# Another order for the first unit of an attention and maxout kernel, with other masks, loads and weight conversion

## The chip, the cores and the metric

The kernel runs on one core of a Trainium2 chip. The metric is the device time of one execution in microseconds (us); lower is better. Engines are named as the profile names them: PE is TensorE (matmuls), DVE is VectorE, ACT is ScalarE, POOL is GpSimd, and SP is SyncE, which here only issues DMAs.

## What is computed

Three stages follow each other: banded attention (4 batches, 8 heads, 576 positions, 64 wide; half of the heads see the last 32 positions, half see every fourth of the last 128), a maxout layer, and a layer with a rational function.

```python
scores = np.where(masks, q @ k.T / 8, -1e9)           # per head
attn = exp(scores - max) / (sum + 1e-9);  x = attn @ v  # (2304, 512)
h = np.maximum(np.maximum(x @ w1, x @ w2), x @ w3)      # (2304, 768)
x = h @ w_out                                           # (2304, 512)
h = x @ w_in                                            # (2304, 2048)
g = (a0 + a1*h + a2*h**2 + a3*h**3) / (1 + abs(b0*h) + abs(b1)*h**2 + 1e-6)
out = g @ w_out2                                        # (2304, 512)
```

The weights arrive as 64-bit floats, and the kernel makes 32-bit ones out of their bits.

## The kernel before, in words

**Tiling.** The 2304 tokens are twelve attention chunks of 192 (c = 0 to 11). Two chunks are a unit u of 384 tokens. For each of the six units `moe1(u)` runs 18 maxout groups (6 values of f by j = 0, 1, 2) and then four output groups `wo1`. Each product is made from high and low halves: per 128 rows of depth three matmuls, high by high, high by low, low by high (`mm3`). A maxout group is 12 matmuls with 384 columns, a wo1 group 18. While unit u is in `moe1`, the attention of unit u + 1 is woven in between. After the six units comes the rational layer.

**Attention of a chunk** has two kinds of heads, p (plain) and d (dilated), and the steps S (scores on PE, with the mask added by a matmul for the first four chunks), MX (row maximum on DVE), E (exponential on ACT, for the first four chunks one instruction per 64 or 48 rows, with the sum read out of an accumulator), SB (division by the sum, DVE), X (transposes on PE and a copy), V (times the values on PE), and VE (split into x1h by ACT and x1l by DVE).

**Conversion of a weight tile** (128x512, 24 tiles for `moe1`): `load`, `abs` on ACT, three passes `bits` on DVE, `hi` on ACT, `lo` on POOL. The `abs` result lives in a buffer `cvt`, of which there are four in unit 0; `lo` frees it. A group of PE reads a tile's `hi` first and its `lo` in its third matmul. In unit 0 and 1 POOL also makes `hl`, the low half of the maxout result. In units 1 to 4, 32 tiles of the last layer's weights are converted and stored by POOL's DMA queue (`w2d`), with two `cvt` buffers.

**Order.** The string START lists by hand what happens before `moe1(0)`, the two chunks of unit 0 and S2:p of unit 1. W:n are n matmuls on zeros that only keep PE busy. Each engine runs its own instructions in that order. All later steps are ordered by a scheduler. All input loads, also those of later chunks, are issued by SP; the load of chunk c + 2's queries stands behind the scores of chunk c, in whose buffer it lands.

## Time and profile before

| | |
|---|---|
| median of 3 runs | 841.38 us (840.77 to 842.07) |
| the profiled execution | 840.17 us, of it 838.4 us span |
| PE busy | 808.7 us (96%) |
| DVE busy | 646.2 us (77%) |
| ACT busy | 488.5 us (58%) |
| POOL busy | 133.8 us (16%) |

The span lies inside the time of the execution, 1.8 us are around it. Busy time is an average over stages; how full an engine is in a stage is read from a table of windows. The granted clock of TensorE is given as a share of 2.4 GHz.

### The profile page before, as it was taken

Reading aid. Unit: us, or ns where it says so; the run is one execution under the profiler, and the core shown is the slowest. Engines: PE = TensorE matmul, PEld = TensorE weight load, DVE = VectorE, ACT = ScalarE, POOL = GpSimd, SP = SyncE. Lnnn points to the kernel's source line nnn. Section 1 sums busy time; section 2 is a strip of 40 time slices with the busy share of each in tenths; the row PEclk is TensorE's granted clock in tenths of the full one; section 3 lists DMA queues with packets and bytes.
Section 4 is the critical chain, followed back from the end, with each engine's and each line's share of the span. In section 5 each row is a group of like instructions: output and inputs, shape, how many; then the busy total and the mean of one; then the engine's idle time right before and its main releaser. Section 6 shows DMA issues by size and latency. Waiting matters only on the chain.

```text
span 838.4 us, 13171 instructions
## 1 busy us (share of the span) xinstructions
PE 808.7 (96%) x4965; PEld 750.4 (89%) x4965; DVE 646.2 (77%) x1172; ACT 488.5 (58%) x1023; POOL 133.8 (16%) x145
## 2 busy tenths in 40 slices
PE   7889789999999999999989999999999999999998
PEld 5688689999999999999988899999999999999996
DVE  4689937657758657636349899999999999998996
ACT  3565622333333333325449788788778778777775
POOL 0156431220010010016860000000000000000000
PEclk9699889999999999999999999999999999999999
DMA  8784313664555544444620002002002001000001
GB/s 284 233 303 152 148 59 119 207 209 156 171 168 160 191 151 127 153 140 150 207 95 1 1 1 76 1 0 76 2 1 76 0 1 38 1 2 7 31 1 38
DMA packets 29439, 82.54 MB, mean 98 GB/s; under 512 B 3904, under 2 KB 7488, under 8 KB 29376
## 3 DMA queue, kind: packets, MB, share of 16 engines
q1 hardware_dynamic: 24080, 64.66, 24.0%
q0 software_dynamic: 5296, 17.04, 5.5%
q8 instruction: 39, 0.64, 0.3%
q14 instruction: 24, 0.20, 0.1%
HBM read 63.87 MB, written 17.83 MB: 97 GB/s over the span
## 4 chain that ended last, share of the span: by engine, by line
PE 86%; issue 5%; POOL 3%; ACT 3%; DVE 3%; DMA 1%; SPq 0%; POOLq 0%; ACTq 0%; DVEq 0%
PE mm L505 10%; PE mm L506 10%; PE mm L504 10%; PE acc L780 8%; PE acc L778 8%; PE acc L779 8%; PE h L505 8%; PE h L504 8%; PE h L506 8%; PE sc L289 3%; POOL w1s L487 2%; PE tpp L345 2%; PE pv L371 1%; PE pv L365 1%; POOL wo1s L487 1%
## 5 line engine op out<-in xcount | busy, mean ns | idle before, releaser
L506 PE MATMUL mm<-x1h,w1s 128*128 128x384 f32 x432 | 147.0, 340 | 3.6 <-POOL w1s L487 3.6
L504 PE MATMUL mm<-x1h,w1s 128*128 128x384 f32 x432 | 149.3, 347 | 0.4 <-ACT w1s L479 0.4
L505 PE MATMUL mm<-x1l,w1s 128*128 128x384 f32 x432 | 146.7, 340 | 1.0 <-DVE x1l L387 1.0
L504 PE MATMUL h<-x2h,w2s 128*128 128x384 f32 x384 | 129.6, 337 | 3.8 <-DVE p L739 3.8
L505 PE MATMUL h<-x2l,w2s 128*128 128x384 f32 x384 | 129.9, 338 | 0.0
L506 PE MATMUL h<-x2h,w2s 128*128 128x384 f32 x384 | 129.8, 338 | 0.0
L778 PE MATMUL acc<-w2s,gh 128*128 128x512 f32 x288 | 113.6, 394 | 0.0
L779 PE MATMUL acc<-w2s,gh 128*128 128x512 f32 x288 | 113.4, 394 | 0.0
L780 PE MATMUL acc<-w2s,gl 128*128 128x512 f32 x288 | 110.3, 395 | 0.0
L729 ACT ACTIVATE q<-h 128x384 f32<-128x384 f32 x96 | 47.2, 491 | 77.6 <-PE h L506 76.2
L736 DVE SCALAR_TENSOR_TENSOR q<-q,cs,ab 128x384 f32<-128x384 f32 x96 | 67.5, 704 | 29.5 <-ACT ab L730 29.4
L506 PEld LDWEIGHTS mm<-x1h,w1s 128*128 128x128 f32 x432 | 82.5, 191 | 5.2 <-POOL w1s L487 5.2
L505 PEld LDWEIGHTS mm<-x1l,w1s 128*128 128x128 f32 x432 | 82.5, 191 | 2.2 <-DVE x1l L387 2.2
L504 PEld LDWEIGHTS mm<-x1h,w1s 128*128 128x128 f32 x432 | 82.3, 191 | 1.3 <-ACT w1s L479 0.7
L504 PEld LDWEIGHTS h<-x2h,w2s 128*128 128x128 f32 x384 | 72.6, 189 | 8.0 <-DVE p L739 4.1
L505 PEld LDWEIGHTS h<-x2l,w2s 128*128 128x128 f32 x384 | 72.5, 189 | 3.8
L506 PEld LDWEIGHTS h<-x2h,w2s 128*128 128x128 f32 x384 | 72.6, 189 | 0.3
L523 DVE TENSOR_TENSOR m<-mm,m 128x384 f32<-128x384 f32 x72 | 39.8, 553 | 42.7 <-PE mm L506 38.8
L731 ACT ACTIVATE p<-h,cs 128x384 f32<-128x384 f32 x96 | 65.1, 678 | 0.0
L780 PEld LDWEIGHTS acc<-w2s,gl 128*128 128x128 f32 x288 | 54.1, 188 | 12.0
L745 ACT ACTIVATE r<-q,cs 128x384 f32<-128x384 f32 x96 | 59.6, 621 | 5.1 <-DVE q L736 4.6
L779 PEld LDWEIGHTS acc<-w2s,gh 128*128 128x128 f32 x288 | 54.1, 188 | 9.4
(90 smaller groups left out, 1588.9 us busy)
## 6 DMA issues: line engine op xcount, KB each, us to landing
w1r<-in_w_dram SPq DMA_DIRECT2D x18, 512.0 KB, 7.5
raw<-in_w_in_dram SPq DMA_DIRECT2D x16, 512.0 KB, 3.8
w2d<-cvt POOLq DMA_DIRECT2D x32, 256.0 KB, 3.4
...
x2d<-xs POOLq DMA_DIRECT2D x24, 192.0 KB, 2.4
```

The costliest lines, as they stand in the source:

```text
L487: nc.gpsimd.tensor_sub(slot[:, 512:1024], t, slot[:, 0:512].bitcast(F32))
L504: nc.tensor.matmul(o, lhsT=lh, rhs=rh, start=(i == 0), stop=False)
L505: nc.tensor.matmul(o, lhsT=lh, rhs=rl, start=False, stop=False)
L506: pe_at[0] = nc.tensor.matmul(o, lhsT=ll, rhs=rh, start=False, stop=(i == n - 1))
L523: nc.vector.tensor_tensor(out=t, in0=o, in1=t, op=ALU.max)
L729: nc.scalar.activation(out=s["q"], in_=s["h"], func=AF.Square)
L731: nc.scalar.activation(out=s["p"], in_=s["h"], func=AF.Identity, scale=cs[:, 3:4], bias=cs[:, 2:3])
L736: nc.vector.scalar_tensor_tensor(out=s["q"], in0=s["q"], scalar=cs[:, 5:6], in1=s["ab"], op0=ALU.mult, op1=ALU.add)
L745: nc.scalar.activation(out=s["r"], in_=s["q"], func=AF.Ln, scale=LS, bias=cs[:, 6:7])
L778: nc.tensor.matmul(o, lhsT=gh, rhs=w[:, 0:512], start=(c == 0), stop=False)
L779: nc.tensor.matmul(o, lhsT=gh, rhs=w[:, 512:1024], start=False, stop=False)
L780: nc.tensor.matmul(o, lhsT=gl, rhs=w[:, 0:512], start=False, stop=(c == F2 - 1))
```

## The change

It has five parts.

1. START is replaced by another list. It has one block W:14 at its head and no later W, runs the scores of both chunks first, splits E, X and VE into smaller steps (D, E, SM; X, XC; VH, VL), and goes on into `moe1(0)`: H:n is the first half (192 columns, chunk 0) of group n, P:n the second half or, from n = 3, the whole group, M, HH and HL what follows on ACT and DVE. It ends behind the sixth group.
2. The masks and the identity come as bf16 constants in two small loads (`mask16`, `maskd16`), and the fp32 identity in one; the three casts go.
3. Loads: in the first unit SP issues only loads into fresh tiles. The queries of chunks 2 to 11, the keys of batches 1 to 3, the values of chunks 2 to 11 and the coefficients go to POOL's queue.
4. A weight's sign and exponent come from one ACT pass (`up`, Prelu with slope -2^32 in place of Abs), so that `bits` has two DVE passes instead of three. `lo` and all `hl` go from POOL to DVE. `cvt` has three buffers instead of four.
5. E writes sums through the accumulator only where EXPS says "A" (0:p, and chunks 2 and 3); chunk 1 sums on DVE, and 0:d uses one subtraction on DVE and one exponential. SB of 0:p multiplies on ACT, six instructions.

```diff
 START = """
-W:7
-S0:p v:0 L:3 S0:d MX0:p E0:p MX0:d S1:p W:2
...
+W:14 kp0 mk16 qp0 kd0 qd0 mkd16 kp1 qp1 qd1 L:1 ident L:1 v0 L:1 L:1 v1 L:1 L:1 L:1 L:1 L:1 rest
+S0:p,sc MX0:p E0:p S0:d,mm MX0:d S1:p,pv D0:d E0:d SB0:p,act SM0:d S1:d,mm MX1:p SB0:d E1:p
...
+VL1:d up VL1:p H:1 up bits up P:0 hi bits P:1 lo hi bits M:0 up H:2 M:1 hi bits P:2 lo hi M:2
+P:3 lo HH:0 HL:0 lo P:4 M:3 M:4 P:5 M:5 HH:1 HL:1
 """
...
-    ACT_UNITS = 4
+    EXPS = {"0:p": "A", "1:p": "C", "1:d": "C", "2:p": "A", "2:d": "A", "3:p": "A", "3:d": "A"}
     MASK_PE = 4
-    HL_POOL = 2
...
-    CVT = 4
+    CVT = 3
...
         if part is None:
-            nc.sync.dma_start(out=kTp, in_=src)
+            nc.gpsimd.dma_start(out=kTp, in_=src)
+            nc.gpsimd.dma_start(out=kTd.rearrange("p n m -> p (n m)"), in_=kd_in[b])
...
+        queue = nc.sync if c < QA else nc.gpsimd
...
+        queue = nc.sync if c < 2 else nc.gpsimd
...
-        nc.scalar.activation(out=t, in_=cv[i][1].bitcast(F32), func=AF.Abs, scale=SHRINK)
+        nc.scalar.activation(out=t, in_=cv[i][1].bitcast(F32), func=AF.Prelu, scale=SHRINK,
+                             alpha=-(2.0 ** 32))
...
-        elif part == 1:
-            nc.vector.scalar_tensor_tensor(out=t, in0=high, scalar=SIGN, in1=t,
-                                           op0=ALU.bitwise_and, op1=ALU.bitwise_or)
...
-            nc.gpsimd.tensor_sub(slot[:, 512:1024], t, slot[:, 0:512].bitcast(F32))
+            nc.vector.tensor_sub(slot[:, 512:1024], t, slot[:, 0:512].bitcast(F32))
...
-                    (nc.gpsimd if u < HL_POOL else nc.vector).tensor_sub(hl, t, hh.bitcast(F32))
```

On ACT, at the start of the program, before the change (sb are the exponentials, spare the same for chunk 1 in the change; pt is a copied transpose, x1h the split result, cvt the weight tile in work, w1s a finished one):

```order
L320 ACTIVATE sb_186,sm_188<-sc_174,mx_187 128x96 x3
L320 ACTIVATE sb_186,sm_188<-sc_175,mx_187 128x96 x3
L320 ACTIVATE sb_217,sm_219<-sc_199,mx_218 96x48 x4
L320 ACTIVATE sb_217,sm_219<-sc_200,mx_218 96x48 x4
L449 ACTIVATE cvt_294<-w1r0_0_193 128x512
L386 ACTIVATE x1h0_172<-pv_278 128x2x192
```

On ACT, at the same place, in the change:

```order
L361 ACTIVATE sb_218,sm_220<-sc_206,mx_219 128x96 x3
L361 ACTIVATE sb_218,sm_220<-sc_207,mx_219 128x96 x3
L357 ACTIVATE sb_248<-sb_248 96x8x48
L379 ACTIVATE sb_218<-sb_218,sm_220 128x96 x6
L361 ACTIVATE spare_203<-sc_253,mx_265 128x96 x3
L361 ACTIVATE spare_203<-sc_254,mx_265 128x96 x3
L397 ACTIVATE pt_319<-tpp_314 48x384
L361 ACTIVATE spare_203<-sc_279,mx_293 96x80 x4
L361 ACTIVATE spare_203<-sc_280,mx_293 96x80 x4
L397 ACTIVATE pt_363<-tpp_328 96x384
L503 ACTIVATE cvt_365<-w1r0_0_174 128x512
L432 ACTIVATE x1h0_204<-pv_343 128x2x4x48
```

The first split result (x1h) now stands behind the exponentials of both chunks, and the eight exponentials of 0:d are one.

On DVE, in the second value of f of `moe1(0)`, in the change (tile names: 533 is conversion tile 5, 629 is 6, 650 is 7, 671 is 8; a row that writes w1s is a `lo`):

```order
L511 SCALAR_TENSOR_TENSOR cvt_533<-w1r1_2_193,cvt_533 128x512
L533 TENSOR_TENSOR w1s1_0_527<-cvt_492,w1s1_0_527 128x512
L509 TENSOR_SCALAR cvt_629<-cvt_629 128x512
L511 SCALAR_TENSOR_TENSOR cvt_629<-w1r2_0_195,cvt_629 128x512
L533 TENSOR_TENSOR w1s2_0_668<-cvt_629,w1s2_0_668 128x512
L509 TENSOR_SCALAR cvt_650<-cvt_650 128x512
L511 SCALAR_TENSOR_TENSOR cvt_650<-w1r2_1_197,cvt_650 128x512
L533 TENSOR_TENSOR w1s2_1_677<-cvt_650,w1s2_1_677 128x512
L571 TENSOR_TENSOR m_531<-mm_535,m_531 128x384
L533 TENSOR_TENSOR w1s1_1_549<-cvt_496,w1s1_1_549 128x512
L509 TENSOR_SCALAR cvt_671<-cvt_671 128x512
```

Before, the `lo` steps stood on POOL, in the order in which PE reads the tiles:

```order
L487 TENSOR_TENSOR w1s1_0_542<-cvt_494,w1s1_0_542 128x512
L487 TENSOR_TENSOR w1s1_1_578<-cvt_503,w1s1_1_578 128x512
L528 TENSOR_TENSOR hl0_603<-m_523,hh0_602 128x384
L487 TENSOR_TENSOR w1s1_2_606<-cvt_545,w1s1_2_606 128x512
L487 TENSOR_TENSOR w1s2_0_668<-cvt_581,w1s2_0_668 128x512
L487 TENSOR_TENSOR w1s2_1_692<-cvt_609,w1s2_1_692 128x512
```

In the change the `lo` of w1s1_1 stands behind those of w1s2_0 and w1s2_1. In the built program the cvt tiles 492, 629, 650 and 671 have one address, so each of them waits for the `lo` of the one before.

POOL's queue at the start, in the change (before, POOL held two casts there and no load):

```order
L648 DMA co_141<-in_a_dram 128x4
L649 DMA co_141<-in_b_dram 128x2
L232 DMA qTp2_216<-in_qp_dram 128x768
L235 DMA qTd2_242<-in_qd_dram 128x768
L217 DMA kTp1_244<-in_kp_dram 128x1152
L218 DMA kTd1_245<-in_kd_dram 128x1152
L232 DMA qTp3_263<-in_qp_dram 128x768
```

These loads now run beside SP's. On PE the last 3572 rows, from inside the wo1 part of unit 0 to the end, are the same before and after apart from buffer numbers.

## Rows read from the trace of the kernel before

**Rows 1.** Windows: us; busy PE, PEld, DVE, ACT, POOL; granted clock; DMA share; GB/s.
```profile
0.00:39.40 39.40, 31.20 (x258) 22.56 (x258) 20.76 (x53) 18.34 (x81) 3.42 (x8) 0.86 0.80 264
39.40:111.90 72.50, 59.81 (x413) 54.71 (x411) 66.98 (x98) 44.31 (x112) 41.03 (x28) 0.90 0.54 189
...
128.90:189.00 60.10, 59.86 (x469) 58.55 (x468) 40.62 (x72) 20.86 (x39) 13.11 (x18) 1.00 0.56 186
...
440.00:838.00 398.00, 393.67 (x1956) 354.89 (x1956) 364.02 (x688) 306.36 (x604) 8.02 (x15) 1.00 0.05 19
```

**Rows 2.** Timeline of PE: start, length, instruction, idle before it and releaser.
```profile
7.82 0.66 PE L280 MATMUL sc<-mP,ident 128*128 128x288 bf16 x2 [3.33 <-POOL ident L589]
...
37.50 1.95 PE L371 MATMUL pv<-pt,vd 80*64 80x48 f32 x32
39.38 0.69 PE L504 MATMUL mm<-x1h,w1s 128*128 128x384 f32 x1
...
55.89 0.69 PE L506 MATMUL mm<-x1h,w1s 128*128 128x384 f32 x1 [1.80 <-POOL w1s L487]
...
59.26 0.36 PE L504 MATMUL mm<-x1h,w1s 128*128 128x384 f32 x1
...
71.16 1.14 PE L371 MATMUL pv<-pt,vd 80*64 80x48 f32 x32
...
124.54 0.33 PE L504 MATMUL mm<-x1h,w1s 128*128 128x384 f32 x1
...
186.87 0.44 PE L504 MATMUL mm<-x1h,w1s 128*128 128x384 f32 x1
```

**Rows 3.** The chain that ended last, around 115 us: start, length, what.
```profile
112.56 0.32 PE mm L504
...
120.02 0.17 PE mm L504
```

**Rows 4.** Timeline of DVE, 44 to 48 us.
```profile
44.19 0.69 DVE L462 SCALAR_TENSOR_TENSOR cvt<-w1r,cvt 128x512 int32<-128x512 int32 x1
44.80 0.42 DVE L459 TENSOR_SCALAR cvt<-cvt 128x512 int32<-128x512 int32 x1
45.13 0.69 DVE L465 SCALAR_TENSOR_TENSOR cvt<-w1r,cvt 128x512 int32<-128x512 int32 x1
...
46.33 0.55 DVE L523 TENSOR_TENSOR m<-mm,m 128x384 f32<-128x384 f32 x1
46.80 1.65 DVE L465 SCALAR_TENSOR_TENSOR cvt<-w1r,cvt 128x512 int32<-128x512 int32 x1
```

**Rows 5.** Timeline of POOL at the same time.
```profile
46.62 1.28 POOL L487 TENSOR_TENSOR w1s<-cvt,w1s 128x512 fp32r<-128x512 f32 x1 [2.76 <-ACT w1s L479]
```

**Rows 6.** Timeline of ACT: first exponentials, and a conversion.
```profile
11.79 0.34 ACT L320 ACTIVATE sb<-sc,mx 128x96 f32<-128x96 f32 x1 [9.77 <-DVE mx L312]
12.03 0.19 ACT L320 ACTIVATION_READ_ACCUMULATOR sb<-sc,mx 128x1 f32 x1
12.12 0.33 ACT L320 ACTIVATE sb<-sc,mx 128x96 f32<-128x96 f32 x1
...
26.06 0.66 ACT L479 ACTIVATE w1s<-cvt 128x512 fp32r<-128x512 f32 x1
26.59 0.68 ACT L449 ACTIVATE cvt<-w1r 128x512 f32<-128x512 f32 x1
27.14 0.51 ACT L349 ACTIVATE pt<-tpp 96x384 f32<-96x384 f32 x1
```

**Rows 7.** Windows of 2 us, columns as in rows 1.
```profile
18.00:20.00 2.00, 2.00 (x37) 1.83 (x36) 1.94 (x9) 1.42 (x5) 0.00 (x0) 1.00 1.01 407
...
26.00:28.00 2.00, 0.30 (x3) 0.30 (x4) 1.67 (x2) 1.65 (x4) 1.19 (x1) 1.00 1.08 246
28.00:30.00 2.00, 1.30 (x8) 0.63 (x6) 1.90 (x5) 1.73 (x9) 0.07 (x1) 0.64 1.01 276
```

**Rows 8.** DMA issues on the page: count, KB each, median us to landing.
```profile
x2d<-xs POOLq DMA_DIRECT2D x24, 192.0 KB, 2.4
```

More of the change, by code (lines that the diff above doesn't have):

```diff
@@ L190, with bank @@
     at_k = {}
+    done_v = {}
+    def bank(pool, name):
+        if pool == "tp":
+            return tp_p.tile([128, 512], F32, tag="tp", name=name)
+        if pool == "sc":
+            return sc_p.tile([128, 512], F32, tag="sc", bufs=2, name=name)
+        return (mm_p if pool == "mm" else pv_p).tile([128, 512], F32, tag=pool, name=name)
     x1 = {}
+    spare = []
     def load_k(b, part=None):
@@ L243, in attn_pieces @@
         kTp, kTd = at_k[b]
+        if c == 0:
+            spare.append(com.tile([128, NP * TU], F32, tag="x1h", bufs=2, name="spare"))
         if part == 0:
@@ L408, in attn @@
             for word in row.replace("-", "").split():
-                word = word.replace("a:", f"{2 * u}:").replace("b:", f"{2 * u + 1}:")
-                if word not in done_words:
-                    do(word)
+                op, _, arg = word.partition(":")
+                for part in parts.get(op[:-1], (op[:-1],)):
+                    do(f"{part}{2 * u + (op[-1] == 'b')}:{arg}")
             yield
@@ L506, in mm3, with m1_mm @@
             pe_at[0] = nc.tensor.matmul(o, lhsT=ll, rhs=rh, start=False, stop=(i == n - 1))
+    m1 = {}
+    def m1_mm(u, f, j, cols=slice(0, TU)):
+        if (u, f, j) not in m1:
+            m1[u, f, j] = mm_p.tile([128, 512], F32, tag="mm", name="mm")[:, 0:TU]
+        x1h, x1l = x1[u]
+        w = w1s[f, j]
+        mm3(m1[u, f, j][:, cols], [(w[:, 128 * c:128 * c + 128], w[:, 512 + 128 * c:640 + 128 * c],
+                                    x1h[:, c, cols], x1l[:, c, cols]) for c in range(KC)])
@@ L530, in moe1 @@
+                if ("P", u, f, j) not in m1_done:
+                    m1_mm(u, f, j)
+                if ("M", u, f, j) not in m1_done:
+                    m1_max(u, f, j)
+                if j == 2 and ("HH", u, f) not in m1_done:
+                    m1_hh(u, f)
+                if j == 2 and ("HL", u, f) not in m1_done:
+                    m1_hl(u, f)
                 yield ("h", f, j)
+        hs = [m1["h", u, f] for f in range(F1)]
         for c in range(KC):
@@ L618 @@
                         cv_step("load")
-                elif op == "v":
-                    load_v(int(arg))
+                elif op in loads:
+                    loads[op]()
                 elif op == "W":
-                    busy(*[x if x.isalpha() else int(x) for x in arg.split(",")])
-                elif op[0] == "b" and op[1:].isdigit():
-                    assert cv_at["bits"] < cv_at["abs"]
-                    cv_bit(cv_at["bits"], int(op[1:]))
-                    cv_at["bits"] += op == "b2"
+                    busy(int(arg))
+                elif op == "H":
+                    m1_mm(0, 0, int(arg), slice(0, CH))
+                elif op == "P":
+                    f, j = divmod(int(arg), 3)
+                    m1_mm(0, f, j, slice(CH if (0, f, j) in m1 else 0, TU))
+                    m1_done.add(("P", 0, f, j))
+                elif op == "M":
+                    f, j = divmod(int(arg), 3)
+                    m1_max(0, f, j)
+                    m1_done.add(("M", 0, f, j))
+                elif op in ("HH", "HL"):
+                    f = int(arg)
+                    (m1_hh if op == "HH" else m1_hl)(0, f)
+                    m1_done.add((op, 0, f))
                 elif op in steps:
@@ L630 @@
                     do(word)
-                    done_words.add(word)
         cs = const.tile([128, 8], F32, name="cs")
```

258 lines of the change are left out of this document (139 added, 119 removed).

## The prediction, made before the result

> **What bounds the kernel now.** I read the windows by stage first. From 128.9 us on PE is busy 59.86 of 60.10 us, and in the last layer 393.67 of 398.00, both at full clock [rows 1]. There only fewer or faster matmuls could help, and the change leaves PE's rows from unit 0's wo1 part to the end as they are. So the gain can only come from the time up to 124.54, where PE begins the first group of unit 1 [rows 2].
>
> That time has two parts. Up to 39.38 [rows 2] attention of two chunks is done step after step, with PE partly on dummy matmuls. From 39.38 to 124.54, 85.2 us, PE does unit 0. What would that cost at full clock? Matmuls with 384 columns follow each other every 0.17 us [rows 3]; alternating 0.17 and 0.18 makes 0.1735. Unit 0 has 18 x 12 + 4 x 18 = 288 of them, 50.0 us. Unit 1 takes 62.3 us (124.54 to 186.87 [rows 2]), so attention woven in costs 12.4 us. Unit 0 thus lost some 23 us to waits and half clock.
>
> The reason is DVE: 66.98 busy us of 72.50 [rows 1]. Its instructions there are of two lengths. Undisturbed, a two-input pass over 128x512 takes 0.61 us from start to start (44.19 to 44.80), the one-input pass 0.33 (44.80 to 45.13), a 128x384 pass 0.47 (46.33 to 46.80) [rows 4]. But the pass that starts at 46.80 lasts 1.65 us [rows 4], and POOL's `lo` runs from 46.62 to 47.90 [rows 5]: the pass ends about 0.6 us after POOL does. Such pairs repeat through the stage. POOL's 41 busy us there [rows 1] cost DVE time of its own.
>
> **When unit 0 can start.** The first score matmul starts at 7.82, after a wait for POOL's cast of the identity [rows 2]. The change has no cast and 160 KB less ahead of this step. I take 1 us off: 6.8. Before, the first exponential came 4.0 us later, at 11.79 [rows 6], with the scores at half clock; fourteen dummy matmuls right up to them should keep the clock, which saves some 1.2 us. First exponential: 9.6.
>
> From there ACT carries the chain. An exponential with accumulator takes 0.33 us (11.79 to 12.12), without one at most 0.24 (11.79 to 12.03); a 512-wide pass takes 0.54 (26.06 to 26.59 to 27.14), and a 384-wide one, 0.51 long [rows 6], some 0.45 in a row. In the change's order ACT does, up to the last x1h of chunk 1: 6 exponentials with accumulator (2.0), one wide one (0.4), 6 + 6 + 8 + 2 short ones (5.2), ten copies or splits (4.5), four conversion passes (2.1): 14.2 us. Without any wait that ends at 23.8. Of this, 8.3 us stand ahead of the first split, at 17.9, and it needs V0:d.
>
> V0:d needs the values of chunk 0. The loads up to them on SP's queue are 4.5 MB. At the 407 GB/s of a full DMA stretch [rows 7] that is 11 us, at 264, the mean of the first stage [rows 1], 17: alone they land between 12 and 18. But POOL's queue sends queries 2 and keys 1 (2.0 MB) at the same time; all of it ahead costs 4.8 us more, so 12 to 23. I take 20, nearer to the shared case, as the DMA engines are full in that stretch. That is 20 + 1.95 for V0:d at half clock [rows 2] = 22.0, 4 us later than ACT wants it. Half clock because PE then idles: before, PE was busy only 0.30 us between 26 and 28, and the clock granted fell to 0.64 in the next window [rows 7]; the 1.95 at 37.50 against 1.14 at 71.16 for the same V step [rows 2] is its price. The V steps of chunk 1 at half clock add some 1.5. H:0, the first group, starts at 23.8 + 4 + 1.5 = **29.3** instead of 39.38; bounds 24 and 33.
>
> The Trainium skill, "DMA: Bandwidth & Descriptors", section "SWDGE vs HWDGE vs iDMA", says that a DMA engine takes turns between the queues fed by POOL and those fed by SP. No row of before has both at once. With strict turns the values would land at about 22, and the total would be 2 us higher.
>
> **Unit 0 from there.** Matmuls: 50.0 us. Three groups are cut into halves of 192 columns; a half lies between half of 0.1735 and all of it, so the cut costs 0 to 6 us. Weight loads of the same size keep up with about 0.1 us in the score steps, so I take 0.1: 1.1 us. Attention of chunks 2 and 3: 12.4, less S2:p (1.5, done ahead), more six mask matmuls (0.8): 11.7.
>
> DVE loses one pass of three per tile (24 x 0.61 = 14.6 us) and gains `lo` and `hl` (24 x 0.61 + 6 x 0.47 = 17.5). That is 3 us more, but POOL no longer computes, so its passes are all undisturbed: per tile 0.33 + 0.61 + 0.61 = 1.55 us.
>
> **A new wait.** On DVE the `lo` of w1s1_1 stands behind those of tiles 6 and 7, and these two, like tile 8, use the one buffer that tile 3 frees. So they run one after the other: `up` 0.54, `bits` 0.94, `hi` 0.54, `lo` 0.61, with hand-overs 3.0 us each, and DVE has nothing else in its queue. From H:0 at 29.3: x1l of chunk 1 is done at 30.3; then three tiles' bits and one `lo` (3.4), SB2:p (1.0), a maximum that waits for group 1 (to 36.2), bits and `lo` of tile 3 (37.8), tiles 6 and 7 (43.8), a maximum (44.3), the `lo` of w1s1_1 (44.9). PE has by then done six halves and group 3 (6 x 1.2 + 2.1, and 1.6 for half clock, from 29.3: 40.2) and two matmuls of group 4. It waits 4.4 us; bounds 2 and 7.
>
> Clock: the wait of 1.80 at 55.89 was followed by eleven matmuls in 3.37 us (to 59.26 [rows 2]), 1.5 more than at full clock. I count this twice, at H:0 and after the new wait: 3.2.
>
> Sum: 29.3 + 50.0 + 1.1 + 11.7 + 4.4 + 3.2 = **99.7** for the start of unit 1, against 124.54. DVE must convert 16 tiles between 44.9 and about 90, when wo1 needs the last: 16 x 1.55 = 25 us, and 13.5 us for maxima, `hl` and attention. 38.5 of 45 us is tight but fits, so PE bounds again.
>
> **What costs nothing.** The coefficients' preparation now stands first on DVE and waits for two tiny loads, but DVE has nothing to do before about 8. Prelu has no row; the nearest is Abs at 0.68 [rows 6]; POOL, DVE and ACT have room for half as much again, since ACT is busy 44.31 of 72.50 [rows 1]. The order has one table load before and after, so no reload is to be priced. In units 1 to 4 DVE is at 40.62 of 60.10 [rows 1] and PE full: the pass that is saved there brings nothing.
>
> **The rivals.** *The early loads don't collide* and the clock stays up: H:0 at 24.5, one slow stretch, unit 1 at 93: 31.5 saved, 810. For it: SP's loads were issued first. Against: the DMA share is 1.0 already with one queue [rows 7].
>
> *The conversion becomes the bound.* With three buffers and in-order queues a tile may cost 2.3 us of DVE's time rather than 1.55: 16 x 2.3 + 13.5 = 50 us from 44.9, the last `lo` at 95, PE done at 105 and with lost clock 107: 824.
>
> *The long passes stay*, because POOL was not their cause: each tile then costs some 1.0 us more, 20 us in all, of which 13 reach the end: 834. The times of rows 4 and 5 speak against it.
>
> *Slower.* POOL's queue now holds loads that wait for PE (queries for the scores two chunks back, values for V) in front of the `w2d` stores. A late store holds one of two cvt buffers, then `up` on ACT, and behind it the copies that free PE's banks. PE idles in none of these units today [rows 1], so each such hold shows fully; above 6.2 us in each of four units the gain is gone, at 8 it is 848. Against: the loads are due half a unit ahead of use. The Trainium skill, "SBUF — State Buffer", section "SBUF: two separate sides", warns that POOL cannot write descriptors while DVE runs certain passes, so its DMAs wait; by that rule these stalls would be likelier, and the time again about 848. POOL's x2d stores land in 2.4 us [rows 8], while DVE is two thirds busy [rows 1], which speaks against it here.
>
> **How the numbers follow.** 124.54 - 99.7 = 24.8 saved. From the profiled execution, 840.17, that leaves 815.3; the median of the runs lies 1.2 higher, so 816.5. Chances: the forecast 0.62 (own range 811 to 821: H:0 3 us and the new wait 2 us to either side), no collision 0.16, conversion bound 0.13, long passes 0.04, slower 0.03, nothing gained 0.02. The range 807 to 826 takes in the first three but their ends. A difference of 0.2%, 1.7 us, is what can be told from none. Faster 0.95, same 0.02, slower 0.03.
>
> **What would show it.** The first maxout matmul near 29 and the first of unit 1 near 100; DVE passes of 1.5 us gone from unit 0; a wait of PE for L533 of 2 to 7 us at the fifth group, and a half clock after it; ACT's first x1h waiting for V0:d, and that for the values. A PE busy share under 98% in units 1 to 4 would make the prediction wrong upward, an H:0 before 25 downward.

## The result, and the profile after

The changed kernel takes 831.3 us (median of 4 runs, 828.4 to 832.1), the kernel before 841.7 (840.8 to 842.2). The ratio is 0.987, with a 95% interval of 0.985 to 0.990. The forecast was 816.5 with a range of 807 to 826: the direction was right, but the gain is 10.4 us where 24.9 were forecast, and the time lies above the range.

The profiled execution of the changed kernel took 828.4 us, 826.6 of it span. Windows by stage, columns as in [rows 1]; the cuts are the first maxout matmul, the first matmul of unit 1, of unit 5, of the rational layer, and the first output matmul of that layer:

```profile
0.00:40.47 40.47, 26.94 (x232) 21.69 (x232) 17.36 (x47) 16.06 (x51) 7.02 (x16) 0.76 0.93 271
40.47:114.29 73.82, 68.86 (x516) 66.58 (x515) 54.45 (x111) 46.93 (x126) 5.93 (x11) 0.92 0.50 186
114.29:365.63 251.34, 250.48 (x1938) 245.11 (x1937) 146.37 (x279) 85.46 (x160) 41.59 (x77) 1.00 0.51 162
365.63:418.73 53.10, 50.77 (x291) 49.92 (x289) 22.12 (x28) 23.84 (x47) 32.87 (x26) 1.00 0.50 158
418.73:435.76 17.03, 15.77 (x87) 14.82 (x87) 12.63 (x14) 13.39 (x27) 12.20 (x10) 1.00 0.26 75
435.76:826.60 390.84, 386.95 (x1931) 348.86 (x1930) 357.88 (x676) 302.02 (x594) 8.03 (x15) 1.00 0.06 19
```

The same windows of the kernel before, where [rows 1] does not have them:

```profile
124.54:375.75 251.21, 250.48 (x1938) 245.40 (x1937) 162.97 (x305) 85.38 (x160) 33.06 (x55) 1.00 0.50 162
375.75:426.35 50.60, 50.36 (x291) 49.91 (x289) 21.94 (x28) 23.86 (x47) 33.52 (x26) 1.00 0.53 166
426.35:446.92 20.57, 16.77 (x88) 16.45 (x87) 16.32 (x16) 14.99 (x29) 11.78 (x10) 0.92 0.21 62
```

Read the second number, the length of each stage. The first stage did not get shorter (40.47 us, before 39.38). Unit 0 did (73.82, before 85.16). Units 1 to 4 are the same to 0.2 us. Then two stages moved that the forecast had held fixed: unit 5 grew by 2.5 us, and the start of the rational layer shrank by 3.5.

The timeline of PE, columns as in [rows 2], shows what holds the first stage and unit 0:

```profile
1.32 6.16 PE L673 MATMUL warmth<-warm 96*128 96x512 bf16 x14 [1.32 <-DVE cs L710]
7.27 0.62 PE L299 MATMUL sc<-mk 128*128 128x288 bf16 x2
9.13 1.55 PE L308 MATMUL sc<-kTp,qTp 128*128 128x96 f32 x12 [1.24 <-DMA qTp<-in_qp_dram]
...
22.83 1.14 PE L415 MATMUL pv<-pt,vd 48*64 48x48 f32 x32 [2.00 <-DMA vd<-in_vd_dram]
...
37.28 1.95 PE L415 MATMUL pv<-pt,vd 80*64 80x48 f32 x32 [7.85 <-DMA vd<-in_vd_dram]
...
40.47 0.53 PE L550 MATMUL mm<-x1h,w1s 128*128 128x192 f32 x1
...
58.44 0.69 PE L552 MATMUL mm<-x1h,w1s 128*128 128x384 f32 x1 [4.96 <-DVE w1s L533]
...
114.29 0.33 PE L550 MATMUL mm<-x1h,w1s 128*128 128x384 f32 x1
```

The large wait is the one at 37.28: PE stands still for 7.85 us until the values of chunk 1 are there, and the first maxout matmul follows at 40.47, for which 29.3 was forecast. The chain of waits (start, length, what) says how late that load is:

```profile
7.62 9.77 DMA w1r<-in_w_dram
17.41 19.74 DMA vd<-in_vd_dram
37.28 1.95 PE pv L415 x32
```

SP issues it at 17.41, behind four weight tiles, and it lands 19.7 us later. The wait at 58.44 is the new wait of the forecast. DVE's timeline ahead of it:

```profile
51.38 0.43 DVE L509 TENSOR_SCALAR cvt<-cvt 128x512 int32<-128x512 int32 x1 [0.73 <-ACT cvt L503]
51.85 0.69 DVE L511 SCALAR_TENSOR_TENSOR cvt<-w1r,cvt 128x512 int32<-128x512 int32 x1
53.30 0.69 DVE L533 TENSOR_TENSOR w1s<-cvt,w1s 128x512 fp32r<-128x512 f32 x1 [0.76 <-ACT w1s L525]
54.71 0.43 DVE L509 TENSOR_SCALAR cvt<-cvt 128x512 int32<-128x512 int32 x1 [0.72 <-ACT cvt L503]
...
57.70 0.68 DVE L533 TENSOR_TENSOR w1s<-cvt,w1s 128x512 fp32r<-128x512 f32 x1
```

Two tiles go through one buffer one after the other, from 51.38 to 54.71 the first of them, and DVE sits idle 0.7 us at each hand-over to ACT; only then, at 57.70, comes the low half that PE wants.

DVE's two-input (L465, L511) and one-input passes (L459, L509) no longer stretch. Two groups by form, 62 to 102 us, with count, busy us, and mean ns; before:

```profile
L465 DVE SCALAR_TENSOR_TENSOR cvt<-w1r,cvt 128x512 int32<-128x512 int32 x10 | 10.1, 1019 | 0.0
L459 DVE TENSOR_SCALAR cvt<-cvt 128x512 int32<-128x512 int32 x13 | 9.3, 726 | 0.0
```

and after:

```profile
L511 DVE SCALAR_TENSOR_TENSOR cvt<-w1r,cvt 128x512 int32<-128x512 int32 x8 | 5.3, 684 | 0.0
L509 DVE TENSOR_SCALAR cvt<-cvt 128x512 int32<-128x512 int32 x13 | 5.1, 420 | 0.3 <-ACT cvt L503 0.3
```

The mean of the two-input pass fell from 1019 to 684 ns, that of the one-input pass from 726 to 420.

### The profile page after: what moved, and what is told of

It reads as the page before. It is cut to its first block, busy times and chain, and to the rows that moved or that the text cites. A ratio compares the mean times of both kernels' runs of the same rounds, so it can differ in the third digit from the quotient of the medians.

```text
span 826.6 us, 13122 instructions
## 1 busy us (share of the span) xinstructions
PE 799.8 (97%) x4986; PEld 747.0 (90%) x4986; DVE 610.8 (74%) x1152; ACT 487.7 (59%) x1002; POOL 107.6 (13%) x155
## 3 DMA queue, kind: packets, MB, share of 16 engines
q1 hardware_dynamic: 18320, 47.37, 18.3%
## 4 chain that ended last, share of the span: by engine, by line
PE 87%; DMA 5%; ACT 2%; DVE 2%; issue 1%; POOL 1%; SPq 1%; ACTq 0%; POOLq 0%; DVEq 0%
PE mm L550 11%; PE mm L551 11%; PE mm L552 11%; PE acc L849 8%; PE acc L851 8%; PE acc L850 8%; PE h L552 8%; PE h L550 8%; PE h L551 8%; PE sc L308 3%; DMA vd<-in_vd_dram 2%; PE tpp L386 2%; PE pv L415 2%; PE pv L409 1%; DMA w1r<-in_w_dram 1%
## 5 line engine op out<-in xcount | busy, mean ns | idle before, releaser
L552 PE MATMUL mm<-x1h,w1s 128*128 128x384 f32 (+1 forms) x444 | 149.3, 336 | 5.0 <-DVE w1s L533 5.0
L550 PE MATMUL mm<-x1h,w1s 128*128 128x384 f32 (+1 forms) x444 | 152.0, 344 | 2.1 <-DVE m L571 2.1
L551 PE MATMUL mm<-x1l,w1s 128*128 128x384 f32 (+1 forms) x444 | 149.2, 336 | 1.0 <-DVE x1l L436 1.0
L552 PEld LDWEIGHTS mm<-x1h,w1s 128*128 128x128 f32 x444 | 85.0, 192 | 5.3 <-DVE w1s L533 5.3
L550 PEld LDWEIGHTS mm<-x1h,w1s 128*128 128x128 f32 x444 | 84.9, 192 | 3.2 <-DVE m L571 2.4
L551 PEld LDWEIGHTS mm<-x1l,w1s 128*128 128x128 f32 x444 | 85.2, 192 | 2.3 <-DVE x1l L436 2.2
L807 DVE SCALAR_TENSOR_TENSOR q<-q,cs,ab 128x384 f32<-128x384 f32 x96 | 65.1, 678 | 29.4 <-ACT ab L801 28.9
L571 DVE TENSOR_TENSOR m<-mm,m 128x384 f32<-128x384 f32 x72 | 40.0, 555 | 46.0 <-PE mm L552 40.7
L850 PEld LDWEIGHTS acc<-w2s,gh 128*128 128x128 f32 x288 | 54.0, 187 | 8.9
L849 PEld LDWEIGHTS acc<-w2s,gh 128*128 128x128 f32 x288 | 54.0, 188 | 8.5
```

The costliest lines, as they stand in the source:

```text
L550: nc.tensor.matmul(o, lhsT=lh, rhs=rh, start=(i == 0), stop=False)
L551: nc.tensor.matmul(o, lhsT=lh, rhs=rl, start=False, stop=False)
L552: pe_at[0] = nc.tensor.matmul(o, lhsT=ll, rhs=rh, start=False, stop=(i == n - 1))
L571: nc.vector.tensor_tensor(out=m1[u, f], in0=o, in1=m1[u, f], op=ALU.max)
L807: nc.vector.scalar_tensor_tensor(out=s["q"], in0=s["q"], scalar=cs[:, 5:6], in1=s["ab"], op0=ALU.mult, op1=ALU.add)
L849: nc.tensor.matmul(o, lhsT=gh, rhs=w[:, 0:512], start=(c == 0), stop=False)
```

## The experiments

All are edits of the changed kernel, unless they say "before"; in the diffs `...` marks what is left out. The lengths in this table (us) are read from the starts of the first matmuls of each stage in each kernel's own trace; a kernel's profile is one of its runs, so the median can lie beside it, and two runs of one kernel can be up to 8 us apart (f1: 809.8 to 817.9).

| kernel | median | first maxout matmul | from there to unit 1 | unit 5 | start of the rational layer |
|---|---|---|---|---|---|
| before | 841.4 to 842.0 | 39.38 | 85.2 | 50.6 | 20.6 |
| changed | 831.3 | 40.47 | 73.8 | 53.1 | 17.0 |
| e1 values first | 830.7 | 35.52 | 74.2 | 54.7 | 21.8 |
| e2 low halves early | 831.6 | 38.43 | 71.8 | 54.5 | 21.6 |
| e3 loads on SP | 824.7 | 32.69 | 76.9 | 54.5 | 17.4 |
| e4 = e1 + e2 | 829.8 | 36.98 | 75.3 | 52.9 | 21.6 |
| e6 last nine low halves on DVE | 829.4 | 39.32 | 74.4 | 53.1 | 15.5 |
| e7 low halves back on POOL | 844.1 | 39.66 | 89.1 | 51.1 | 20.6 |
| e8 order | 824.5 | 40.96 | 67.5 | 53.0 | 21.4 |
| e9 = e3 + e6 + e8 | 816.5 | 30.87 | 73.7 | 53.2 | 14.6 |
| g1 before, low halves on DVE | 834.0 | 40.76 | 73.2 | 52.9 | 21.3 |
| g2 before, one-pass signs | 837.9 | 43.70 | 78.1 | 50.6 | 20.6 |
| f1 = e9 + interleaved loads | 813.5 | 29.43 | 68.7 | 53.4 | 14.6 |
| f2 = e9 + early input load | 814.9 | 29.46 | 72.9 | 53.7 | 15.1 |
| f4 = f1, all low halves on DVE | 810.1 | 30.67 | 69.8 | 50.6 | 14.6 |
| h1 same bytes ahead, on SP | 833.3 | 42.76 | 72.2 | 57.0 | 20.6 |
| h2 = f1 + more dummy matmuls | 817.0 | 32.37 | 70.1 | 56.4 | 14.6 |

In all of them units 1 to 4 take 249 to 252 us, and the rest of the rational layer takes 390.8 to 391.5.

### The late values

Values ahead of the weight tiles:

```diff
-... qd1 L:1 ident L:1 v0 L:1 L:1 v1 L:1 L:1 L:1 L:1 L:1 rest
+... qd1 ident v0 v1 L:1 L:1 L:1 L:1 L:1 L:1 L:1 L:1 L:1 rest
```

> Theory: what the sum missed are the values of chunk 1. In the changed kernel their load stands on SP's queue behind four weight tiles, is issued at 17.41 us and lands 19.7 us later, and PE stands for 7.85 us before V1:d. Here SP issues the values of both chunks before the first weight tile. Both should have landed by 25 us, the wait of PE before V1:d should fall from 7.85 us to under 1, the first maxout matmul start near 31 us instead of 40.47, and the time be about 822 us. Rival 1: the DMA engines are full, so the weight tiles come later by what the values come earlier; then the first maxout groups wait for a weight load, H:0 starts at 36 us or later, and the time is 826 to 829. Rival 2: the half clock and not the values sets the pace: 831, as the changed kernel.

Measured: 830.7 us (829.9 to 831.3); the waits of PE for values are gone, but the first maxout matmul came at 35.52. ACT's timeline says why:

```profile
26.60 0.67 ACT L503 ACTIVATE cvt<-w1r 128x512 f32<-128x512 f32 x1 [2.83 <-DMA w1r<-in_w_dram]
...
29.30 0.67 ACT L503 ACTIVATE cvt<-w1r 128x512 f32<-128x512 f32 x1 [0.61 <-DMA w1r<-in_w_dram]
```

The weight tiles now come late, and behind these waits in ACT's queue stand the copies that V1:d needs. That is close to rival 1: what SP issues last comes late, while POOL's loads run beside it. Unit 1 still began 4.6 us earlier (109.74), yet the time stayed: unit 5 and the start of the rational layer took 6.4 us more than in the changed kernel. That sent the study to the tail, below.

All later queries, keys and values back to SP's queue:

```diff
-            nc.gpsimd.dma_start(out=kTp, in_=src)
+            nc.sync.dma_start(out=kTp, in_=src)
...
-        queue = nc.sync if c < QA else nc.gpsimd
+        queue = nc.sync
...
-        queue = nc.sync if c < 2 else nc.gpsimd
+        queue = nc.sync
```

> All loads of queries, keys and values go back to SP's queue, behind the first nine weight tiles; POOL's queue loads only the coefficients. Theory A: the values of chunk 1 land late because POOL's queue (queries 2 and 3, keys 1: 2.7 MB by 20 us) shares the DMA engines with SP's. Then they land about 8 us earlier, near 29 us, and the first maxout matmul starts near 32. What it does to the end is open, since the later loads on SP wait for PE: 823 if no weight tile is late, 835 if the weight tiles behind those loads are. Theory B: the place on SP's own queue, behind four weight tiles, and the pace of issue set the landing: the values of chunk 1 still land after 34 us, the first maxout matmul starts at 38 us or later, and the time is 830 to 840.

Measured: 824.7 us (823.1 to 825.3). The values of chunk 1, issued at 16.73, land at 29.4 instead of 37.15, although they stand at the same place of SP's queue (issues from 16.6 to 17.2 us, with KB and us to landing):

```profile
vd<-in_vd_dram SPq DMA_DIRECT2D x1, 320.0 KB, 12.6
```

V1:d starts 0.1 us after them:

```profile
29.50 1.95 PE L415 MATMUL pv<-pt,vd 80*64 80x48 f32 x32 [2.48 <-DVE x1l L436]
```

The profile puts its wait down to x1l, which ended at the same time as the values landed, so either can be what released it. Theory A holds: the first maxout matmul is at 32.69, 7.8 us earlier. So what POOL's queue brings at that time costs the values nearly 8 us. Is it the queue, or only its bytes? Here the same loads stand on SP ahead of the values:

```diff
-... v0 L:1 L:1 v1 L:1 L:1 L:1 L:1 L:1 rest
+... v0 L:1 L:1 rest
-... S1:d,mm MX1:p ...
+... S1:d,mm v1 L:1 L:1 L:1 L:1 L:1 MX1:p ...
```

(on top of e3; the queries and keys are issued at the steps S, which now come before v1).

> As the kernel with all loads on SP, but the loads of queries 2 and 3 and keys 1 (2.7 MB) stand on SP's queue ahead of the values of chunk 1 and five weight tiles behind them; POOL's queue stays empty. Theory A, the bytes count: at the 300 GB/s of that stretch they cost the values 7 to 9 us, which land at 36 us or later (29.3 with the loads behind), as with the loads on POOL's queue (37.1), and the first maxout matmul starts at 38 us or later. Theory B, POOL's queue is what takes the share: without it the values land before 33 us, and the first maxout matmul starts before 36.

Measured: 833.3 us (830.1 to 836.2). The values were issued at 24.47 and landed at 37.3, as with POOL's queue:

```profile
vd<-in_vd_dram SPq DMA_DIRECT2D x1, 320.0 KB, 12.8
```

The first maxout matmul came at 42.76, with the scores of the next chunks pulled ahead of it, which adds some 2 us of its own. Theory A holds: the bytes count, whichever queue carries them. The Trainium skill, "DMA: Bandwidth & Descriptors", section "SWDGE vs HWDGE vs iDMA", lets a DMA engine take turns between the two kinds of queue; that is compatible with both runs, and neither shows it by itself.

### The new wait

Low halves of the second f ahead of the maximum of group 2:

```diff
-... hi bits P:2 lo hi M:2
-P:3 lo HH:0 HL:0 lo P:4 ...
+... hi bits P:2 lo lo hi lo M:2
+P:3 HH:0 HL:0 P:4 ...
```

> Theory: the new wait of PE for the low half of the second tile of the second f (4.96 us) comes from DVE's order alone, since that step stands behind the conversion of two later tiles that share one buffer. Here the low halves of the second f stand ahead of the maximum of group 2 in the written order, and in DVE's order directly after each other. The wait should be under 1 us, the half clock behind it (about 1.5 us) go too, and the time be 825 us. Rival 1: DVE or the three buffers set the pace of the conversion, and PE waits the same 5 us for a tile one to four groups later: 830 to 832. Rival 2: the maximum of group 2, now behind three low halves, holds a PSUM bank, and PE loses 2 to 3 us there: 828.

Measured: 831.6 us (829.9 to 835.4). The wait of 4.96 us is gone, and a wait of 2.55 us for the maximum (L571) came in its place, as rival 2 has it; unit 0 is 2.0 us shorter, and the tail, 5.9 us longer, took it. The two edits together:

> The edits of the two kernels before together: the values ahead of the weight tiles, and the low halves of the second f ahead of the maximum. Theory: the two waits are independent and their gains add: first maxout matmul near 31 us, no wait over 1 us in the first six groups, 816 us. Rival: with unit 0 begun 9 us earlier, the conversion (DVE, with three buffers) or the weight loads cannot keep up, and half of the two gains is lost in waits for weight tiles after the sixth group: 822 to 824.

Measured: 829.8 us (827.6 to 834.2). The gains don't add, and less is left of them than even the rival had: from the first maxout matmul to unit 1 it is 75.3 us, with a wait of 2.54 for the maximum and one of 2.34 for an exponential. Next, maximum first, then the low halves, and only then the seventh tile:

```diff
-... hi bits P:2 lo hi M:2
-P:3 lo HH:0 HL:0 lo P:4 ...
+... hi bits P:2 lo hi M:2
+lo lo up P:3 HH:0 HL:0 bits P:4 ...
```

> In the written order the maximum of group 2 and then the low halves of the second f's second and third tile stand ahead of the conversion of the seventh tile, so that DVE does not take the seventh and eighth tile first. Theory: both the wait for that low half (4.96 us in the changed kernel) and the one for the maximum (2.55 us in the kernel that had moved the low halves ahead of it) go; the way from the first maxout matmul to unit 1 falls from 73.8 us to 67 to 68.5, and the time is 825 to 826, if the rational layer starts as in the changed kernel. Rival: the seventh and eighth tile now come late, and PE waits for them 3 us or more after the sixth group: 72 us and 830.

Measured: 824.5 us (822.3 to 826.8). Neither wait is there any more, and the way to unit 1 is 67.5 us, as expected: 6.3 us less for another order of the same steps. So the wait and its half clock were as large as forecast, and it was DVE's order that made them.

### POOL beside DVE

Low halves from the seventh weight tile on back on POOL:

```diff
-            nc.vector.tensor_sub(slot[:, 512:1024], t, slot[:, 0:512].bitcast(F32))
+            (nc.gpsimd if i >= 6 else nc.vector).tensor_sub(slot[:, 512:1024], t, slot[:, 0:512].bitcast(F32))
```

> From the seventh weight tile on, the low half goes back to POOL (1.28 us there, 0.61 on DVE); the first six tiles and the list START stay as in the changed kernel. Theory: POOL's passes make DVE's long again. DVE gives up 18 passes of 0.61 us (11 us), but passes of 1.2 to 1.7 us come back, and from 62 us on, where DVE is busy 36.5 of 39.3 us, the conversion gets slower: PE waits for weight tiles, unit 1 starts 77 us or more after the first maxout matmul (73.8 in the changed kernel), and the time is 834 to 840. Rival: the long passes come back but hide behind PE, which was busy without a gap from 62 us on: unit 1 starts 73 to 75 us after the first maxout matmul, 830 to 832. Rival 2: the passes are not long, since POOL was not their cause: DVE has 11 us less to do, and the time is 829 to 831 with DVE's passes at 0.7 us.

Measured: 844.1 us (839.5 to 847.2), slower than before the change (ratio 1.003, interval 1.001 to 1.006). The groups by form, 62 to 102 us:

```profile
L509 DVE TENSOR_SCALAR cvt<-cvt 128x512 int32<-128x512 int32 x14 | 10.0, 718 | 2.4 <-ACT cvt L503 2.4
L511 DVE SCALAR_TENSOR_TENSOR cvt<-w1r,cvt 128x512 int32<-128x512 int32 x9 | 9.9, 1107 | 0.1
L511 DVE SCALAR_TENSOR_TENSOR cvt<-wo1r,cvt 128x512 int32<-128x512 int32 x6 | 8.0, 1329 | 0.1
```

DVE's passes are long again, 718 and 1107 to 1329 ns instead of 420 and 684, although DVE has less to do. PE waits 4.1 us for a copied transpose on ACT, which stands behind a conversion that waits 1.7 us for POOL's low half, and 5.3 us for an exponential, ahead of which ACT waits 2.9 us for DVE's row maximum; unit 1 starts 89.1 us after the first maxout matmul. The theory holds, with a larger price than it named; how much of it is DVE's longer passes and how much the buffers that POOL's own pass holds longer was not separated.

The same from the other side, in the kernel before: low halves on DVE, three passes as before.

```diff
-    HL_POOL = 2
+    HL_POOL = 0
...
-            nc.gpsimd.tensor_sub(slot[:, 512:1024], t, slot[:, 0:512].bitcast(F32))
+            nc.vector.tensor_sub(slot[:, 512:1024], t, slot[:, 0:512].bitcast(F32))
```

> The kernel before with one part of the change alone: the low halves of the weight tiles and of the maxout result on DVE instead of POOL (three passes per tile for the bits as before). Theory: POOL's passes are what makes DVE's long, so DVE's work per tile falls although it gets more of it: 0.33 + 2 x 0.61 + 0.61 = 2.2 us undisturbed, against a sum with passes of 1.2 to 1.7 us before; unit 0 takes 76 to 80 us instead of 85.2, and the time is 832 to 837. Rival: DVE was busy 67.0 of 72.5 us there and gets 17.5 us of work more, which the shorter passes do not pay: unit 0 takes 88 us or more, 844 to 850.

Measured: 834.0 us (830.8 to 834.2), ratio 0.990 (0.988 to 0.992). This part alone takes unit 0 from 85.2 to 73.2 us, all that the whole change brought there. In 62 to 102 us DVE's passes take 684 and 420 ns in it, as in the changed kernel, with three passes per tile and four `cvt` buffers as before: so it is POOL's passes that make DVE's long. And the one-pass signs alone, in the kernel before:

```diff
-        nc.scalar.activation(out=t, in_=cv[i][1].bitcast(F32), func=AF.Abs, scale=SHRINK)
+        nc.scalar.activation(out=t, in_=cv[i][1].bitcast(F32), func=AF.Prelu, scale=SHRINK,
+                             alpha=-(2.0 ** 32))
...
-        for part in range(3):
-            cv_bit(i, part)
+        cv_bit(i, 0)
+        cv_bit(i, 2)
```

> The kernel before with another part of the change alone: sign and exponent from one Prelu pass on ACT, so that DVE makes two passes per tile instead of three; low halves stay on POOL. Theory: with POOL's passes as they were, a DVE pass that falls together with one still ends with it, so taking one pass away gives back less than its 0.61 us per tile (24 tiles, 14.6 us): 836 to 839. Rival: DVE's amount of work is all that counts: unit 0 is shorter by 10 us or more, 828 to 831. Rival 2: Prelu costs ACT more than Abs (0.68 us a pass) and ACT becomes late: 842 or more.

Measured: 837.9 us (837.7 to 838.0). DVE's passes stay long (1125 and 775 ns in 62 to 102 us), and unit 0 is 7.1 us shorter, about half of the 14.6 us taken away, as the theory has it. That the time lies in its range is luck in part: the first maxout matmul comes 4.3 us later than before, which the theory didn't have, and why was not tried.

### The tail

At the start of the rational layer DVE's first pass has two inputs in SBUF, and POOL makes low halves of weights (L619). DVE in the changed kernel:

```profile
422.90 5.34 DVE L807 SCALAR_TENSOR_TENSOR q<-q,cs,ab 128x384 f32<-128x384 f32 x1 [14.07 <-ACT ab L801]
428.17 0.55 DVE L809 TENSOR_TENSOR p<-h,p 128x384 f32<-128x384 f32 x1
...
429.51 1.64 DVE L807 SCALAR_TENSOR_TENSOR q<-q,cs,ab 128x384 f32<-128x384 f32 x1 [0.15 <-ACT ab L801]
```

and POOL there:

```profile
420.27 7.55 POOL L619 TENSOR_TENSOR w2s<-w2r,w2s 128x512 fp32r<-128x512 f32 x6
428.19 4.12 POOL L619 TENSOR_TENSOR w2s<-w2r,w2s 128x512 fp32r<-128x512 f32 x3 [0.37 <-ACT w2s L618]
```

The first pass ends 0.4 us after POOL's series of six; the second, inside POOL's next three, takes 1.64 us. In e1 the series has nine passes, and DVE and POOL read:

```profile
419.69 9.02 DVE L807 SCALAR_TENSOR_TENSOR q<-q,cs,ab 128x384 f32<-128x384 f32 x1 [14.07 <-ACT ab L801]
```

```profile
417.05 11.23 POOL L619 TENSOR_TENSOR w2s<-w2r,w2s 128x512 fp32r<-128x512 f32 x9
```

PE then waits 3.77 us and goes on at half clock. The kernel before had the same long pass and wait (20.6 us in the table): in the changed kernel's profile POOL's series broke off early, because its input came late, and that gave 3.5 us. The last nine low halves on DVE:

```diff
-        nc.gpsimd.tensor_sub(t[:, 512:1024], r, t[:, 0:512].bitcast(F32))
+        (nc.vector if late else nc.gpsimd).tensor_sub(t[:, 512:1024], r, t[:, 0:512].bitcast(F32))
...
-            load_w2(w2c)
+            load_w2(w2c, True)
```

> The low halves of the last nine tiles of the rational layer's weights (loaded behind unit 5) are made on DVE instead of POOL; all else as in the changed kernel. Theory: at the start of the rational layer DVE's first pass takes 5.34 us in the changed kernel and 9.02 in the one with the values first, against 0.61 later on, because it does not end before POOL pauses, and POOL has six to nine low halves in a row there (7.55 and 11.23 us). Without them the pass takes about 0.6 us, the wait of PE for DVE's L810 at that place (0.56 to 3.77 us and half clock behind it) is under 0.6, the first output matmul comes 17 us or less after the first matmul of the layer (17.0 in the changed kernel, 21.7 with the values first, 20.6 before the change), and the time is 826 to 828, with less spread. Rival 1: five of the moved passes stand ahead of DVE's first pass and wait for loads; they delay it by as much: 831. Rival 2: the long pass is a wait for its input: it stays above 5 us.

Measured: 829.4 us (826.5 to 829.8). DVE's timeline:

```profile
419.17 3.10 DVE L619 TENSOR_TENSOR w2s<-w2r,w2s 128x512 fp32r<-128x512 f32 x5 [11.12 <-ACT w2s L618]
422.19 0.61 DVE L807 SCALAR_TENSOR_TENSOR q<-q,cs,ab 128x384 f32<-128x384 f32 x1
```

The pass takes 0.61 us, the wait is gone, and the stage takes 15.5 us. The theory holds; the median is a little above its range (826 to 828).

Unit 5 was next. First by the order of its loads:

```diff
-    LATE_X2 = 200
+    LATE_X2 = 0
```

> The kernel with three edits (816.5 us) and one more: the loads of the rational layer's input stand on SP behind 5 instead of 13 loads of its weights, as far as the order of before had them (7). Theory: unit 5 took 53.1 us in the changed kernel and 50.6 before, because ACT waits 4.0 us for that input (2.6 before), DVE's maximum comes late and PE waits 2.09 us for it. Here unit 5 takes 50.5 to 51.5 us instead of 53.2, and the time is 814. Rival: the wait of PE comes from the long passes that POOL gives DVE at that place, not from the load: unit 5 stays at 53 us, 816 to 817.

Measured: 814.9 us (814.4 to 815.1), which the spread of e9 (812.4 to 819.1) doesn't tell from no gain, and unit 5 took 53.7 us. The wait for the maximum is gone, but PE waits 0.70 and 1.28 us for ACT's first copies of a maximum (L569) instead; ahead of the second, ACT waits 3.18 us for a weight load. So the unit stayed as long as the rival has it, and the edit moved the wait rather than removing it. DVE and POOL in that unit:

```profile
370.42 2.83 DVE L633 TENSOR_TENSOR x2l<-x2r,x2h 128x384 fp32r<-128x384 f32 x2
...
369.98 10.03 POOL L619 TENSOR_TENSOR w2s<-w2r,w2s 128x512 fp32r<-128x512 f32 x7 [2.21 <-ACT w2s L618]
```

DVE's passes take 1.4 us here, beside POOL's. So all 32 low halves went to DVE (with the interleaved loads of f1, below):

```diff
-        nc.gpsimd.tensor_sub(t[:, 512:1024], r, t[:, 0:512].bitcast(F32))
+        nc.vector.tensor_sub(t[:, 512:1024], r, t[:, 0:512].bitcast(F32))
```

> The kernel with the interleaved loads (813.5 us), and the low halves of all 32 tiles of the rational layer's weights on DVE instead of the last nine; POOL makes no pass beside DVE's any more. Theory: the 2.5 us that unit 5 takes longer since the change come from long DVE passes (1.4 to 2.8 us beside POOL's instead of 0.5) between ACT's copies and the maxima: unit 5 takes 50.2 to 51 us instead of 53.4, and the time is 811. Rival 1: DVE's new passes wait in order for loads and delay the maxima by as much: unit 5 53 us or longer, 813 to 816. Rival 2: ACT, waiting for loads, is what is late: 53 us, 813.

Measured: 810.1 us (807.2 to 811.7). Unit 5 and the start of the rational layer, in windows:

```profile
351.06:401.62 50.56, 50.32 (x291) 50.00 (x289) 28.04 (x51) 24.26 (x47) 1.63 (x3) 1.00 0.52 166
401.62:416.21 14.59, 14.59 (x85) 14.59 (x85) 13.08 (x24) 13.80 (x28) 0.54 (x1) 1.00 0.27 86
```

Unit 5 is back at 50.6 us without POOL's passes. That they made it long by making DVE's long is not shown, though, and the traces speak against it. SP's timeline from the start of unit 5 to the load of the rational layer's input (x2r), in the changed kernel and in the kernel before:

```profile
372.01 11.79 SPq L616 DMA_DIRECT2D w2r<-w2d  x8
383.97 0.53 SPq L626 DMA_DIRECT2D x2r<-x2d  x1
```

```profile
382.13 1.89 SPq L549 DMA_DIRECT2D w2r<-w2d  x2
386.61 0.53 SPq L559 DMA_DIRECT2D x2r<-x2d  x1
```

Eight weight loads instead of two stand ahead of it (five more were issued before unit 5 in both), so it is issued 18.3 us into the unit instead of 10.9. In the changed kernel ACT waits for it, and the maximum and PE behind ACT:

```profile
388.95 1.76 ACT L632 ACTIVATE x2h<-x2r 128x384 fp32r<-128x384 f32 x4 [4.00 <-DMA x2r<-x2d]
...
391.53 0.44 PE L550 MATMUL mm<-x1h,w1s 128*128 128x384 f32 x1 [2.09 <-DVE m L571]
```

The three DVE passes between the two take 0.50 us each. All twelve kernels in which SP has this order take 52.9 to 57.0 us for unit 5, and in each PE's wait is 1.9 us shorter than ACT's (3.36 to 6.29 us). The three with the order of before (before, e7, g2) take 50.6 to 51.1, with the same 23 POOL passes and as many long DVE passes. So the order of SP's loads, which the scheduler changed, made unit 5 longer. In f4, x2r is issued 13.7 us into the unit and ACT waits 1.44; that DVE's shorter passes free the buffers of the weight loads sooner would explain it, but is only argued.

### Put together

e3, e6 and e8 in one kernel:

> Three edits together: later queries, keys and values on SP's queue (measured alone at 824.7 us), the last nine low halves of the rational layer on DVE, and the order of the kernel before. Theory: the three work in different stretches and add up: first maxout matmul near 32.7 us, unit 1 near 101, no long pass at the start of the rational layer, 813 to 816 us. Rival: after an earlier start the weight loads or the conversion set the pace in unit 0 and half of the order's gain is lost: 817 to 820.

Measured: 816.5 us (812.4 to 819.1), between the theory and the rival. The first maxout matmul is at 30.87; but PE waits 4.69 us for an exponential at 54 us, behind a conversion on ACT that waits 5.32 us for a weight load: eight loads of chunks 2 and 3 now stand ahead of it on SP. So they were made to take turns with weight tiles:

```diff
-... v1 L:1 L:1 L:1 L:1 L:1 rest
-S0:p,sc MX0:p E0:p S0:d,mm MX0:d S1:p,pv D0:d E0:d SB0:p,act SM0:d S1:d,mm ...
+... v1 L:1 L:1 rest
+S0:p,sc L:1 MX0:p E0:p S0:d,mm L:1 MX0:d S1:p,pv L:1 D0:d E0:d SB0:p,act SM0:d S1:d,mm L:1 ...
-... V0:d,pv
+... V0:d,pv L:1
-... V0:p,mm SM1:d ...
+... V0:p,mm L:1 SM1:d ...
```

> The kernel with three edits (816.5 us) and one more: on SP's queue weight tiles 7 to 12 and the loads of queries, keys and values of chunk 2 and 3 take turns, instead of eight such loads in a row between the ninth and the tenth tile. In the kernel with three edits ACT waits 5.32 us for the tenth tile's load at 49 us and PE 4.69 us at 54 us. Theory: that wait of PE falls under 1.5 us, unit 1 starts near 101 instead of 104.6, and the time is 812 to 814. Rival: the loads of chunk 2 now land late for its scores, or the values of chunk 1 do, and PE loses as much there: 816 to 818.

Measured: 813.5 us (809.8 to 817.9). The wait is 1.72 us, and unit 1 starts at 98.09 (e9: 104.56); the two medians lie within each other's spread. Last, more dummy matmuls for the clock, on top of f1:

```diff
-W:14 kp0 ...
-S0:p,sc L:1 MX0:p ...
+W:18 kp0 ...
+S0:p,sc W:3 L:1 MX0:p ...
```

> The kernel with the interleaved loads (813.5 us), with 18 instead of 14 dummy matmuls at the start and three more behind the first scores, so that PE has no gap before the scores. In that kernel the first scores started at 9.13 us after a gap of 2.46 us and ran at half clock (2.85 us instead of 1.55). Theory: the scores of chunk 0 and 1 run at full clock; each of the four score steps is 1.1 us shorter, two or three of them on the path: the first maxout matmul starts near 27 instead of 29.4, and the time is 811. Rival: the exponentials on ACT set the pace from the first scores on, and the values of chunk 0 land at 21 to 22 us: first maxout matmul at 29, 813. Rival 2: the dummy matmuls end after the first queries have landed and delay the scores: 30 us or later, 814.

Measured: 817.0 us (810.6 to 817.2). The first scores did run at full clock (1.55 us), but the first maxout matmul came at 32.37, with PE waiting 2.71 us for the values of chunk 0 and 1.17 for those of chunk 1. The theory fell: this clock isn't what sets the start. Whether the kernel is slower than f1 the spreads don't tell. Its profile has a wait of 3.88 us for a maximum in unit 5, behind a wait of 5.82 us of ACT for x2r.

The fastest kernel is f4: 810.1 us against 841.8 before, a ratio of 0.962 (0.960 to 0.965), and 2.6% under the changed kernel.

## Why the prediction was wrong, step by step

In the profiled execution the forecast was 815.3 us and the time 828.4, a miss of 13.1. By stage: first maxout matmul +11.2 (40.47 for 29.3), unit 0 +3.4 (73.8 for 70.4), units 1 to 4 +0.1, unit 5 +2.5, start of the rational layer -3.5, rest -0.6. The other runs lie up to 3.7 us higher; they have no trace, and that the start of the rational layer costs them its 3.5 us would fit, but is only argued.

**The failed step is the start of unit 0**, "the V steps of chunk 1 at half clock add some 1.5". The step put the bytes ahead of the values of chunk 0 on the queues, landing at 20 with bounds of 12 and 23, and they landed at 22.70, inside them; V0:d itself then took 1.14 us, at full clock, and not the 1.95 of half clock. The step gave the values of chunk 1 no landing time at all. They stand behind those on SP, with two more weight tiles between, and with POOL's loads beside, and they landed at 37.15, after PE had waited 7.85 us for them. The same sum, made for that load, would have shown most of it. SP's loads up to it are 6.2 MB, and POOL's issued by then 2.0 MB; 8.2 MB at the 264 GB/s of the stage [rows 1] are 31 us. By 37.15 some 10 MB had come in all (271 GB/s in this stage), so loads issued behind the values took part of the rate. e3 and h1 show that POOL's bytes are the cause: without them the values land at 29.4, with the same bytes on SP at 37.3. The rival that the early loads don't collide had it the wrong way round.

**The first exponential** came at 11.59 (forecast 9.6, before 11.79 [rows 6]). The clock held (1.55 us for the scores), but they waited 1.24 us for the queries, until 9.13: the change issues the mask ahead of the queries, which landed at 8.99, and at 4.63 before. So the microsecond that I took off for the masks went the other way. The 2.0 us are not part of the 11.2, since V1:d waited for the values much longer.

**Unit 0 from its start** was priced nearly right. The new wait was 4.96 us (forecast 4.4, bounds 2 and 7), for the reason given, and e8 shows that DVE's order makes it. The clock was put at 3.2: the 72 half matmuls took 10.4 us (40.47 to 50.85) instead of the 8.0 at their full-clock pace of 0.111, and the twelve behind the wait 3.94 (58.44 to 62.38) instead of 2.1, together 4.2. A half costs 0.111 us, not 0.10, so the cut costs 1.8 us where 1.1 was taken (72 x 0.10 less 36 x 0.1735 would even be 0.95). Wait, clock and cut are 2.3 of the 3.4 us; 1.1 stays unassigned.

**POOL as the cause of long passes** was right, and taking its passes away is the change's main gain: g1 gets all of unit 0's 12 us with that part alone, and e7, without it, is slower than before. How much of the 12 us comes from DVE's shorter passes, and how much from the low half itself (0.68 us on DVE, 1.55 on POOL in 62 to 102 us), was not separated. The new order at the start gained nothing in the changed kernel, where the first maxout matmul came 1.1 us later than before; the late values hid its gain, which e3 shows: 6.7 us earlier than before.

**The tail** was held fixed because PE's rows there are the same. They are, but the rows of the other engines and queues are not. In unit 5 SP has other loads ahead of the rational layer's input, which costs the 2.5 us. At the start of that layer, how many POOL passes run in a row beside DVE's first pass is decided by when loads arrive: with POOL's passes the stage takes 17.0 to 21.8 us, without them 14.6 to 15.5. That the changed kernel's profile was short there is luck.

**The rivals.** The conversion did not become the bound (DVE 54.45 of 73.82 us), beyond the wait of 4.96. The slower one fell: units 1 to 4 take 251.34 us, before 251.21, and the x2d stores land in 2.5 us, with loads in the same queue. Three sums among the working are off, without changing the outcome: long passes with 13 us of loss make 829.5 and not 834; the 2.0 MB of POOL at 264 GB/s are 7.5 us and not 4.8, so the upper bound for the values of chunk 0 is nearer 25; and DVE, busy 66.98 of 72.50 us, had no room for half as much again.
